# Four more weight pieces begun in the first five attention groups of an attention, expert and MLP kernel on Trainium2

## Chip, core and metric

The kernel runs on one NeuronCore of a Trainium2 chip (trn2). The metric is the device time of one execution in microseconds (us). Of the kernel before there are three timed runs: 333.08, 333.13 and 334.42 us, median 333.13 us.

## What is computed

Three steps follow each other. All inputs are float32.

```python
def _attn_ref(q, k, v, mem_k, mem_v):          # q, k, v: 4 x 8 heads x 768 x 64
    ...
    chunk, left_ctx, right_ctx = (32, 16, 8)    # 24 chunks of 32 queries, each sees
    ...                                         # 8 memory keys + its own 56 neighbours
        a = softmax(scale * q_c @ k_full.T)
        out[:, :, c_start:c_end] = a @ v_full

def _moe_ref(x, phi, w1, w2):                   # x: 3072 x 512, 8 experts, 4 slots each
    logits = x @ phi
    slot_input = softmax(logits, 0).T @ x       # 32 x 512, needs every token
    slot_out[e] = relu(slot_input[e] @ w1[e]) @ w2[e]     # 512 -> 1024 -> 512
    return softmax(logits, 1) @ slot_out

def _moe2_ref(x, w_in, w_out, g_ln):            # 512 -> 1024 -> 512
    h = x @ w_in
    solu = h * softmax(h)
    return (layernorm(solu) * g_ln) @ w_out
```

## The kernel before

**Attention, 32 groups.** `GROUPS` is 32: four batches, two halves of the sequence, four pairs of heads. The loop over `g` (lines 842 to 874) takes one group per turn. Its keys and queries come as one tile, `kq` (128 x 800, four buffers), its values as two transfers into `vz` (64 x 780 each, four buffers). `emit_spread` copies keys and memory keys into a padded tile `kz` on POOL, with a part on ACT (line 303 is POOL's copy), then TensorE (PE) multiplies queries and keys (line 254), DVE and ACT make the softmax, PE turns it (line 292) and multiplies by the values (line 310). Every fourth group the logits and the running weighted sum for the expert slots are brought up to date. After the last group some merging follows (lines 875 to 912), and only then is the input of the experts known.

**Experts, 32 units.** The loop over `units` (lines 931 to 951) goes through `w1` and `w2` of the eight experts in halves. A unit uses two pieces of 512 KB: eight matmuls at line 497 (`w1`) or at line 515 (`w2`). Between them lie the turn of the hidden values (line 504), a sum on DVE (507) and a relu on ACT (508).

**Last stage.** The 32 slot outputs go through `w_in`, and then 24 tiles of 128 tokens through SoLU, layer norm and `w_out`. Its main matmuls are at line 723.

**Weight pieces.** `chunks` lists 80 pieces of 512 KB in the order of loading: eight of `w_in` (line 234, into `e` areas) alternating with seven of `w_out` (line 234, into `w` areas), then the 64 of the experts (line 231), then the last of `w_out`. `load_e(n)` begins at most `n` more of them, as far as slots are free. A slot of `w_in` becomes free when a cast on POOL (line 592, one of five steps of a cast that is spread over the groups from g = 3 to 30) has read it. When the attention ends, the areas of `kq`, `vz` and of the token tiles become 13 more slots (`ex` areas). From then on a slot becomes free when a unit has used it (`release`, line 941).

**The queue.** Every load is issued by SyncE (SP), in program order: `load_qk(g + 4)`, `load_e(LOADS[g])`, `load_v(g + 3)` in each group. An issue waits until its buffer is free, and everything behind it waits too. SP also has a limit on the transfers under way, as its waits for earlier transfers in the trace show. `LOADS` (line 45) gives the number of pieces per group.

```python
            if g + 4 < GROUPS:
                load_qk(g + 4)
            load_e(LOADS[g])
            if 1 <= g:
                emit_pv(g - 1)
            if g + VLEAD < GROUPS:
                load_v(g + VLEAD)
```

Of the kernel before, what the change touches and what calls it, by code (L numbers as in the profile page):

```python
# [41 lines left out]
NE = 25  # L42
CAST0, CASTN, NEARLY = 3, 3.4, 8
VLEAD = 3
LOADS = [0] + [1, 1, 1, 0] + [1] * 28
LANE, SIDE = 2.6, 1

CASTU = (0, 1, 2, 3, 4, 5, 6)
# [31 lines left out]
def tile_kernel(ctx: ExitStack, tc: tile.TileContext, kr, vr, w1, w2, w_in, w_out, cst, out):  # L80
# [106 lines left out]
    def load_qk(g):  # L187
        sp.dma_start(out=kq[g % 4], in_=kr[g])
# [30 lines left out]
    def load_e(n=99):  # L219
        while n and nxt[0] < len(chunks):  # L220
            key = chunks[nxt[0]]
            if key[0] == "wout":
                slot = wslot[key[1]]
            elif free:
                slot = free.pop(0)
            else:
                break
            slot_of[key] = slot
            if key[0] in ("w1", "w2"):
                src = (w1 if key[0] == "w1" else w2)[key[1], key[2]]  # L230
                sp.dma_start(out=slot.rearrange("p (k f) -> p k f", k=2), in_=src)
            else:
                src = (w_in if key[0] == "win" else w_out)[key[1]]
                sp.dma_start(out=slot.bitcast(I64), in_=src)
            nxt[0] += 1
            n -= 1
# [561 lines left out]
    with tc.manual_schedule():  # L798
# [42 lines left out]
        for g in range(GROUPS):  # L841
# [6 lines left out]
# [4 lines that stand above are left out]
# [207 lines left out]
```

## Time and profile before

| what | value |
|---|---|
| timed runs, median of 3 | 333.13 us |
| profiled execution, its own time | 334.36 us |
| its span in the trace | 332.5 us |
| granted TensorE clock, mean | 0.999 of full speed |
| busy: PE, DVE, ACT, POOL | 90%, 72%, 67%, 51% of the span |
| moved by the DMA engines | 95.86 MB, mean 288 GB/s |
| chain that ended last | PE 56%, DMA 32%, DVE 5% of the span |

The span is the part between the first and the last instruction; 1.86 us of the profiled execution lie around it. Times in rows are microseconds from the span's start. A share of busy time says little here, since the kernel has stages with different limits: the rows further down are read by stage. The GB/s of a stretch is what all 16 DMA engines moved in it.

### The profile page before, as it was taken

How to read it: one execution, taken by the hardware profiler on the slowest of the kernel's cores; microseconds unless marked ns; L12 is line 12 of the kernel's file. 1: busy time of each engine (PE TensorE's matmuls, PEld its weight loads, DVE VectorE, ACT ScalarE, POOL GpSimd, SP SyncE). 2: the span in 40 equal slices, each digit the busy share in tenths (PEclk: the TensorE clock that was granted, in tenths of full speed). 3: DMA queues.
4: the chain of work that ended last, by engine and by line, in shares of the span. 5: the costliest groups of instructions: out<-in, count | busy, mean ns of one | idle time of the engine just before them, and what ended most of it. 6: DMA issues, size and time to landing. Idle time of an engine off the chain costs nothing.

```text
span 332.5 us, 8398 instructions
## 1 busy us (share of the span) xinstructions
PE 300.8 (90%) x3069; PEld 218.1 (66%) x3069; DVE 239.4 (72%) x432; ACT 223.1 (67%) x441; POOL 169.9 (51%) x398
## 2 busy tenths in 40 slices
PE   2979698897897789888999999999999999999996
PEld 2667576675675533332434788888888888888885
DVE  6686887797768438999117886897888778787540
ACT  3476656764765427685524779998888888888721
POOL 5436567566767023222100357777767677676600
PEclk9999999999999999999999999999999999999999
DMA  7999999999999999999950004667666756666531
GB/s 286 366 359 405 407 399 411 412 411 414 409 407 396 418 417 419 415 421 416 417 228 0 0 34 158 252 206 264 207 244 211 246 209 201 240 231 234 202 95 64
DMA packets 39433, 95.86 MB, mean 288 GB/s; under 512 B 4832, under 2 KB 15456, under 8 KB 39392
## 3 DMA queue, kind: packets, MB, share of 16 engines
q1 hardware_dynamic: 39248, 95.11, 75.3%
q8 instruction: 24, 0.39, 0.5%
q10 hardware_dynamic: 144, 0.22, 0.2%
q14 instruction: 17, 0.14, 0.1%
HBM read 78.53 MB, written 16.78 MB: 287 GB/s over the span
## 4 chain that ended last, share of the span: by engine, by line
PE 56%; DMA 32%; DVE 5%; ACT 2%; issue 2%; POOL 1%; SPq 1%; ACTq 0%; POOLq 0%
PE bank L723 37%; DMA kq_area<-in_kr_dram 19%; DMA ex_area<-in_w_dram 6%; DMA e_area<-in_w_dram 6%; PE h L635 4%; PE bank L254 3%; PE bank L310 2%; PE bank L497 1%; POOL kq_area L303 1%; PE bank L292 1%; DMA vz_area<-in_vr_dram 1%; PE bank L515 1%; PE bank L733 1%; PE t L733 1%; PE t L692 1%
## 5 line engine op out<-in xcount | busy, mean ns | idle before, releaser
L723 PE MATMUL bank<-wh_area,yh_area 128*128 128x512 f32 x552 | 129.8, 390 | 0.0
L723 PEld LDWEIGHTS bank<-wh_area,yh_area 128*128 128x128 f32 x552 | 103.4, 188 | 21.8
L303 POOL TENSOR_SCALAR kq_area<-kq_area 64x416 f32<-64x416 f32 x88 | 38.5, 443 | 38.5 <-DMA kq_area<-in_kr_dram 27.9
L254 PE MATMUL bank<-kq_area 128*32 128x128 f32 x768 | 29.8, 293 | 16.8 <-POOL kq_area L303 10.8
L706 DVE STREAM_TRANSPOSE yq_area<-yq_area 128x1024 f32<-128x1024 f32 x20 | 24.9, 1246 | 17.2 <-DMA yq_area<-z 17.2
L254 PEld LDWEIGHTS bank<-kq_area 128*32 128x32 f32 x768 | 21.0, 116 | 23.1 <-POOL kq_area L303 15.2
L650 DVE SCALAR_TENSOR_TENSOR eb_area<-h,eb_area 128x1024 f32<-128x1024 f32 x24 | 29.0, 1213 | 9.2 <-ACT eb_area L644 9.0
L295 ACT COPY s_area<-bank 128x384 f32<-128x384 f32 x32 | 15.2, 476 | 27.7 <-PE bank L292 26.1
L310 PE MATMUL bank<-vz_area,s_area 128*32 128x130 f32 x768 | 29.7, 279 | 2.2 <-ACT s_area L295 1.6
L272 DVE TENSOR_REDUCE cst_area<-bank 128x6 f32<-128x384 f32 x32 | 17.7, 554 | 19.2 <-PE bank L254 19.0
L688 POOL TENSOR_SCALAR cst_area<-cst_area 128x1 f32<-128x1 f32 x72 | 26.6, 369 | 7.6
L641 DVE TENSOR_REDUCE cst_area<-h 128x1 f32<-128x1024 f32 x24 | 29.0, 1216 | 0.9 <-PE h L635 0.9
L644 ACT ACTIVATE eb_area<-h,cst_area 128x1024 f32<-128x1024 f32 x24 | 26.6, 1110 | 1.9 <-DVE cst_area L641 1.9
L673 ACT ACTIVATE eb_area<-eb_area,cst_area 128x1024 f32<-128x1024 f32 x24 | 27.3, 1138 | 0.1
L677 POOL TENSOR_SCALAR cst_area<-cst_area 128x1 f32<-128x1 f32 x24 | 15.9, 662 | 21.7 <-ACT eb_area L644 19.8
L717 DVE TENSOR_TENSOR yh_area<-yq_area,yh_area 128x1024 fp32r<-128x1024 f32 x20 | 24.5, 1224 | 2.3 <-ACT yh_area L713 2.3
L670 ACT ACTIVATE eb_area<-eb_area,cst_area 128x1024 f32<-128x1024 f32 x20 | 23.1, 1155 | 4.3 <-DVE eb_area L650 3.8
L310 PEld LDWEIGHTS bank<-vz_area,s_area 128*32 128x32 f32 x768 | 22.3, 111 | 5.0 <-ACT s_area L295 2.8
L689 POOL TENSOR_SCALAR cst_area<-cst_area 128x1 f32<-128x1 f32 x72 | 21.9, 304 | 7.1
L713 ACT CAST yh_area<-yq_area 128x1024 fp32r<-128x1024 f32 x20 | 21.0, 1049 | 6.3 <-DVE yq_area L706 6.3
L741 ACT ACTIVATE eb_area<-bank,cst_area 128x512 f32<-128x512 f32 x23 | 15.8, 685 | 8.8 <-POOL cst_area L679 5.9
L299 ACT COPY kq_area<-kq_area 64x416 f32<-64x416 f32 (+1 forms) x34 | 12.2, 407 | 11.2 <-DMA kq_area<-in_kr_dram 11.1
(154 smaller groups left out, 534.2 us busy)
## 6 DMA issues: line engine op xcount, KB each, us to landing
e_area<-in_w_dram SPq DMA_DIRECT2D x37, 512.0 KB, 8.5
ex_area<-in_w_dram SPq DMA_DIRECT2D x26, 512.0 KB, 10.0
kq_area<-in_kr_dram SPq DMA_DIRECT2D x32, 400.0 KB, 6.3
vz_area<-in_vr_dram SPq DMA_DIRECT2D x64, 195.0 KB, 6.3
z<-eb_area SPq DMA_DIRECT2D x20, 512.0 KB, 2.7
yq_area<-z SPq DMA_DIRECT2D x80, 128.0 KB, 2.9
out_dram<-eb_area SPq DMA_DIRECT2D x23, 256.0 KB, 2.1
e_area<-in_w_in_dram SPq DMA_DIRECT2D x8, 512.0 KB, 6.4
```

The costliest lines, as they stand in the source:

```text
L254: pe.matmul(out=bk[32 * j:32 * j + 32, t * 128:(t + 1) * 128], lhsT=kq[i][:, KT + c * CH:KT + (c + 1) * CH], rhs=kwin(g % 2, c), start=Tru ...
L303: pool.tensor_scalar(out=o, in0=i, scalar1=1.0, scalar2=0.0, op0=ALU.mult, op1=ALU.add)
L310: pe.matmul(out=bk[32 * j:32 * j + 32, t * 2 * VW:(t + 1) * 2 * VW], lhsT=atb[g % 2][:, c * CH:(c + 1) * CH], rhs=vz[g % 4][:, :, c * VW:( ...
L641: dve.tensor_reduce(out=sc("nm", i), in_=fin["h"][i % 2], axis=AX.X, op=ALU.max, negate=True)
L644: act.activation(out=eb[i % FIN], in_=fin["h"][i % 2], func=ACTF.Exp, bias=sc("nm", i), accum_out=sc("s", i))
L650: dve.scalar_tensor_tensor(out=ub[i % FIN], in0=fin["h"][i % 2], scalar=-1.0 / FF, in1=eb[i % FIN], op0=ALU.mult, op1=ALU.mult, accum_out= ...
L670: act.activation(out=yb[i % FIN], in_=ub[i % FIN], func=ACTF.Identity, scale=-float(FF), bias=sc("nu", i))
L673: act.activation(out=sq, in_=ub[i % FIN], func=ACTF.Square, scale=-float(FF), bias=sc("nu", i), accum_out=sc("vs", i))
L688: pool.tensor_scalar(out=t, in0=r, scalar1=r, scalar2=xx, op0=ALU.mult, op1=ALU.mult)
L706: dve.transpose(out=yv[i % FIN].rearrange("p (f a t) -> p a f t", f=FC, a=4), in_=yq[i % FIN].rearrange("p (a f t) -> p a f t", f=FC, a=4),)
L717: dve.tensor_tensor(out=yl[i % FIN][:, sl], in0=tps(i, sl) if i < NPE else yv[i % FIN], in1=yh[i % FIN][:, sl].bitcast(FP32), op=ALU.subtract,
L723: pe.matmul(out=fin["o"][i % 2], lhsT=a[i % FIN][:, f * 128:(f + 1) * 128], rhs=w[f], start=start, stop=stop)
```

## The change

Only the table `LOADS` changes. Counted from g = 0, the groups g = 1, 2 and 3 begin two pieces each in place of one, and g = 4 begins one in place of none. All later groups begin one as before, so that each piece comes four places earlier in the loop, 34 pieces are asked for in the loop in place of 30, and four fewer are left for after it. No other engine's order changes.

```diff
-LOADS = [0] + [1, 1, 1, 0] + [1] * 28
+LOADS = [0, 2, 2, 2] + [1] * 28
```

SP's queue at the groups g = 1 to 3, before (`e1` is the area of `w_in` pieces, `w0` of a `w_out` piece; `kq` and `vz` belong to groups four and three ahead):

```order
L234 DMA e1_area_73<-in_w_in_dram 128x512
L202 DMA vz_area_71<-in_vr_dram 64x780 x2
L188 DMA kq_area_70<-in_kr_dram 128x800
L234 DMA w0_area_76<-in_w_out_dram 128x512
L202 DMA vz_area_71<-in_vr_dram 64x780 x2
L188 DMA kq_area_70<-in_kr_dram 128x800
L234 DMA e1_area_73<-in_w_in_dram 128x512
```

and with the change:

```order
L234 DMA e1_area_73<-in_w_in_dram 128x512
L234 DMA w0_area_76<-in_w_out_dram 128x512
L202 DMA vz_area_71<-in_vr_dram 64x780 x2
L188 DMA kq_area_70<-in_kr_dram 128x800
L234 DMA e1_area_73<-in_w_in_dram 128x512
L234 DMA w1_area_77<-in_w_out_dram 128x512
L202 DMA vz_area_71<-in_vr_dram 64x780 x2
L188 DMA kq_area_70<-in_kr_dram 128x800
L234 DMA e1_area_73<-in_w_in_dram 128x512
```

In both excerpts the rows of `kq` are the keys of g = 6 and g = 7. Ahead of the keys of g = 6 now stand two pieces in place of one, ahead of those of g = 7 four in place of two.

SP's queue at the end of the attention, from the keys of the last group on, before (`e1`, `e2` are slots that `w_in` pieces had, `ex0` is the area of `kq`):

```order
L188 DMA kq_area_70<-in_kr_dram 128x800
L231 DMA e1_area_73<-in_w2_dram 128x1024
L202 DMA vz_area_71<-in_vr_dram 64x780 x2
L231 DMA e1_area_73<-in_w2_dram 128x1024
L202 DMA vz_area_71<-in_vr_dram 64x780 x2
L231 DMA e1_area_73<-in_w1_dram 128x1024 x2
L231 DMA e2_area_74<-in_w2_dram 128x1024 x2
L231 DMA e2_area_74<-in_w1_dram 128x1024 x2
L231 DMA ex0_area_1696<-in_w2_dram 128x1024 x2
```

and with the change:

```order
L188 DMA kq_area_70<-in_kr_dram 128x800
L231 DMA e2_area_74<-in_w2_dram 128x1024
L202 DMA vz_area_71<-in_vr_dram 64x780 x2
L231 DMA e2_area_74<-in_w2_dram 128x1024
L202 DMA vz_area_71<-in_vr_dram 64x780 x2
L231 DMA e2_area_74<-in_w1_dram 128x1024 x2
L231 DMA ex0_area_1700<-in_w2_dram 128x1024 x2
```

Behind the last keys stand four pieces for slots that are free already or soon, before eight: the other four now lie ahead of these keys. The pieces from `ex0` on have the same places after as before.

## Rows read from the trace of the kernel before

**Rows 1.** The page, what the DMA engines moved, in 40 slices of 8.3 us

```profile
GB/s 286 366 359 405 407 399 411 412 411 414 409 407 396 418 417 419 415 421 416 417 228 0 0 34 158 252 206 264 207 244 211 246 209 201 240 231 234 202 95 64
```

**Rows 2.** Busy time by stretch; last: granted clock, DMA share, GB/s

```profile
14.00:22.00 8.00, 7.74 (x191) 6.15 (x183) 6.18 (x17) 5.89 (x15) 2.40 (x6) 1.00 0.94 317
22.00:100.00 78.00, 66.83 (x1464) 52.31 (x1459) 60.92 (x156) 50.78 (x140) 50.62 (x90) 1.00 1.03 408
...
123.00:166.00 43.00, 38.87 (x312) 14.22 (x305) 32.99 (x73) 28.85 (x68) 11.62 (x13) 1.00 1.03 418
```

**Rows 3.** The chain that ended last, in order of time: start, us, what

```profile
42.86 5.62 DMA kq_area<-in_kr_dram
...
87.79 7.04 DMA kq_area<-in_kr_dram
...
161.61 9.74 DMA e_area<-in_w_dram
171.40 1.05 PE bank L515 x4
```

**Rows 4.** The page's DMA issues: KB each, median us to landing

```profile
kq_area<-in_kr_dram SPq DMA_DIRECT2D x32, 400.0 KB, 6.3
vz_area<-in_vr_dram SPq DMA_DIRECT2D x64, 195.0 KB, 6.3
```

**Rows 5.** SP's queue in order of time, from 9 to 18 us: start, us

```profile
9.63 0.43 SPq L234 DMA_DIRECT2D e_area<-in_w_in_dram  x1
12.88 1.12 SPq L202 DMA_DIRECT2D vz_area<-in_vr_dram  x2
...
17.49 0.43 SPq L234 DMA_DIRECT2D e_area<-in_w_in_dram  x1
```

**Rows 6.** DMA issues at 0.72, 9.63 and 17.49 us; last: us to landing

```profile
kq_area<-in_kr_dram SPq DMA_DIRECT2D x1, 400.0 KB, 4.0
...
e_area<-in_w_in_dram SPq DMA_DIRECT2D x1, 512.0 KB, 5.4
...
e_area<-in_w_in_dram SPq DMA_DIRECT2D x1, 512.0 KB, 7.2
```

**Rows 7.** POOL and PE in order of time, end of attention and first expert unit

```profile
101.36 2.12 POOL L303 TENSOR_SCALAR kq_area<-kq_area 64x416 f32<-64x416 f32 x4 [0.23 <-DMA kq_area<-in_kr_dram]
103.57 1.31 POOL L592 TENSOR_TENSOR cst_area<-e_area,cst_area 128x512 f32<-128x512 f32 x1
...
122.31 1.92 PE L497 MATMUL bank<-e_area,cst_area 128*32 128x512 f32 x16 [0.27 <-DVE cst_area L426]
```

**Rows 8.** SP's queue in order of time: three issues that waited for a slot

```profile
104.91 0.33 SPq L231 DMA_DIRECT2D e_area<-in_w_dram  x1
...
123.40 0.80 SPq L231 DMA_DIRECT2D e_area<-in_w_dram  x2
...
129.91 1.28 SPq L231 DMA_DIRECT2D e_area<-in_w_dram  x3
```

**Rows 9.** DMA issues at 104.91, 123.40 and 129.91 us; last: us to landing

```profile
e_area<-in_w_dram SPq DMA_DIRECT2D x1, 512.0 KB, 8.8
...
e_area<-in_w_dram SPq DMA_DIRECT2D x1, 512.0 KB, 7.7
...
e_area<-in_w_dram SPq DMA_DIRECT2D x1, 512.0 KB, 7.4
```

**Rows 10.** PE by line, 122 to 172 us: busy, mean ns, idle before

```profile
L515 PE MATMUL bank<-e_area,hr_area 128*32 128x512 f32 x76 | 12.7, 604 | 0.9 <-ACT hr_area L508 0.5 <-DMA e_area<-in_w_dram 0.2
```

**Rows 11.** All engines in order of time, the last expert units

```profile
163.87 1.07 PE L515 MATMUL bank<-ex_area,hr_area 128*32 128x512 f32 x8
...
168.04 1.97 PE L515 MATMUL bank<-e_area,hr_area 128*32 128x512 f32 x8
...
168.40 0.22 ACT L508 ACTIVATE hr_area<-hr_area 128x16 f32<-128x16 f32 x1 [1.51 <-DVE hr_area L507]
...
170.24 2.21 PE L515 MATMUL bank<-e_area,hr_area 128*32 128x512 f32 x8 [0.24 <-DMA e_area<-in_w_dram]
```

## The prediction

> **What bounds the kernel now.** I read the page's slices first: the DMA engines move some 410 GB/s from the fourth slice to the twentieth, then nothing, and after that only the last stage's own traffic [rows 1]. So there are two parts: up to about 171 us the loads run at one level, behind them PE works alone. The chain that ended last says the same: in the attention it consists of transfers of `kq` one behind the other, in the expert units of weight pieces, up to a piece issued at 161.61 us that lands 9.74 us later, at 171.35; the four matmuls that wait for it end at 171.40 + 1.05 = 172.45 us [rows 3]. Behind 172.45 us neither the order nor the loads change, so I take these 332.5 - 172.45 = 160.1 us as fixed and ask only when the last expert unit ends.
>
> Next I read the DMA rate by stretch. From 22 to 100 us it is 408 GB/s, from 123 to 166 us 418, but from 14 to 22 us only 317 [rows 2]. That is the gap into which the four pieces are put. SP shows its cause: it issues a `w_in` piece at 9.63 us, waits, and issues the next transfers only at 12.88 us [rows 5], so that few are under way afterwards.
>
> Third, whether the expert units wait for loads. From 122 to 172 us the group of line 515 idled 0.2 us for a transfer [rows 10]. Inside units 31 and 32 it did wait: eight matmuls take 1.07 us in an undisturbed unit, here 1.97 and 2.21 us, and the second starts 2.20 us after the first [rows 11]. So the units run at the engines' own pace almost to the end and meet the loads only in the last two. Two ends lie close together, and the change moves them in opposite directions.
>
> **Part 1: the attention gets later.** A group of the loop loads 400 KB of keys, 2 x 195 KB of values [rows 4] and 512 KB of a piece [rows 6], 1302 KB. In the chain, `kq` transfers follow from the issue at 42.86 us to the landing of that issued at 87.79 us, at 94.83 us: eight links, each from the keys of one group to those of the group two further, 16 groups in 51.97 us, 3.25 us per group [rows 3]. One piece therefore costs 512 / 1302 x 3.25 = 1.28 us of the loads, and four more pieces ahead of the last keys 5.1 us. From this goes what the gap gives back, which I call y. The spread of the last keys on POOL begins at 101.36 us, 0.23 us after POOL is free, when the keys have landed [rows 7]; from there to the first expert unit at 122.31 us is a chain of compute, so that unit begins 5.1 - y later.
>
> **Part 2: what the gap gives back.** The old profile doesn't show this, so I bound it. Below: the deeper queue helps nothing, y = 0. By the rate: 8 us at 317 in place of 408 GB/s are 8 x 91 / 408 = 1.8 us. By landings: the piece issued at 9.63 us lands after 5.4 us, at 15.0; that issued at 17.49 us after 7.2 us, at 24.7 [rows 5, 6]. Between them are two groups' loads, worth 2 x 3.25 = 6.5 us, and they took 9.7: 3.2 us lost. A landing counts the slowest of 16 engines and a rate their mean, hence the two figures; the attention waits for landings, but part of their delay may be slow single transfers that a longer queue doesn't cure. I take 2.4 us, just under the middle of 1.8 and 3.2; the ends are 0 and 3.2.
>
> So the expert units begin 5.1 - 2.4 = 2.7 us later.
>
> **A rule that speaks against it.** The row of 408 GB/s was said above [rows 2]. The Trainium skill, page "DMA: Bandwidth & Descriptors", section "Bandwidth", holds that between HBM and SBUF the memory's share of about 358 GB/s per core binds. By that the gap would give back only 8 x (358 - 317) / 358 = 0.9 us. The end would then be 5.1 - 0.9 - 2.3 = +1.9 us by the steps below. The trace disagrees: two long stretches lie at 408 and 418 GB/s, so the sum stays with the rows.
>
> **Part 3: the compute end of the units.** With no wait for a load, the unit that begins at 168.04 us would end after 1.07 us, at 169.11; the relu that the last unit needs is done at 168.62 us, so the last would end at 170.18 us [rows 11]. Against 172.45 us that is 2.3 us of room. A start 2.7 us later uses it up: the end by compute is 2.7 - 2.3 = 0.4 us later than now.
>
> **Part 4: the load end of the units.** Left alone, the loads are earlier by y, 2.4 us. But three issues wait for compute: one at 104.91 us for the cast of a `w_in` piece on POOL, which ends at 104.88; one at 123.40 us for the first unit; one at 129.91 us for the sixth [rows 7, 8]. They move 2.7 us back while the queue ahead of them drains 2.4 us sooner, which takes 5.1 us from the reserve of each. The reserve is what the piece had to stand in line for: it landed 8.8, 7.7 and 7.4 us after issue [rows 9]. A first transfer of 400 KB with nothing ahead took 4.0 us [rows 6]; 112 KB more at the above pace add 0.3. So the reserves are 4.5, 3.4 and 3.1 us; the smallest lets 5.1 - 3.1 = 2.0 us of idle loads arise in all (idle time at an earlier one counts towards the next). The load end is 2.0 - 2.4 = -0.4 us: earlier than now. Issuing costs SP 0.43 us per piece [rows 5], the same pieces as before, only elsewhere.
>
> The places of PE, DVE, ACT and POOL in their queues don't change. Their waits inside the attention grow with the keys' delay and are part of the 2.7 us already. Slots of `w_in` pieces are asked for four places earlier; the last of them is the wait at 104.91 us, costed above.
>
> **The sum.** The later of the two ends counts: +0.4 us. The profiled execution took 334.36 us, 1.86 us of them around its span, and would take 334.8. That execution stands 1.2 us above the median of 333.13, so against the median I forecast 333.13 + 0.4 = **333.5 us**. A measurement of this kernel can tell about 0.5%, 1.7 us, from no change.
>
> **Rivals.**
> - *The attention is simply pushed back* (slower). If the gap is no lack of queued work, y is near 0 and the units begin up to 5.1 us later: 5.1 - 2.3 = +2.8 us, 335.9. It decides from y below 1.1, where the end passes +1.7. For it: at 17.49 us a piece already takes 7.2 us to land, so something was queued, and the DMA share was 0.94 [rows 2, 6]. Against: the rate climbs to 408 with the same mix of transfers. Chance 0.10.
> - *The gap has a ceiling of its own* (slower). If the rate there rises only halfway, to 362 GB/s, y is 8 x 45 / 362 = 1.0 and the end 5.1 - 1.0 - 2.3 = +1.8 us, 334.9. For it speaks the high DMA share at the low rate, against it the 408 GB/s right behind [rows 2]: chance 0.03. The Trainium skill's page "DMA: Bandwidth & Descriptors" would put such a ceiling near 358 GB/s.
> - *The loads are the end after all, by the slot waits.* If a piece needs 5.4 us to land even with little ahead, as the one at 9.63 us did [rows 6], the smallest reserve is 7.4 - 5.4 = 2.0 us, the idle loads are 3.1 us and the end is 3.1 - 2.4 = +0.7 us, 333.8. Chance 0.17.
> - *The gap is filled entirely* (earlier). With y = 3.2 the units begin 1.9 us later, inside their room: 1.9 - 2.3 = -0.4 us by compute, 2.0 - 3.2 = -1.2 by loads; 332.7. To be over 0.5% faster both ends would have to move 1.7 us, for which the units would also need over a microsecond more room than the rows show. Chance 0.18, of which 0.04 over 0.5%.
> - *Nothing is begun earlier*, because SP comes to its limit of transfers under way at once. Then SP waits where it issued before, and the time is within 0.3 us of 333.1. Against: between 9.63 and 12.88 us SP waits for the multiplication by the values, not for transfers. Chance 0.05.
>
> The forecast's own case has 0.47.
>
> **How the numbers follow.** The first two rivals are slower by over 0.5%, 0.04 of the fourth is faster by that, all else lies within it: faster 0.04, same 0.83, slower 0.13. The range reaches from the full gap, 332.7, less 0.4 us (the next unit's matmuls may begin before the last of a unit has ended, so the room of 2.3 us is a lower bound), up to +2.1 us, y = 0.7, which leaves out most of the first rival: 332.3 to 335.2.
>
> **What would show it.** Right: from 14 to 22 us over 380 GB/s; the first unit of line 497 begins near 125.0 us; units 31 and 32 take close to 1.07 us each; the last matmul of line 515 ends near 172.9; PE's last stage is as long as before. Rival one: the gap's rate stays near 317 and the first unit begins at 126 us or later. The slot waits: a dip of the rate around 127 to 136 us, and the last units still wait for a piece. Wrong altogether: a last stage of another length, or an attention end that doesn't move with the landing of the last keys.

## The result and the profile after

| kernel | time, median | ratio to before | 95% interval |
|---|---|---|---|
| before | 333.12 us | | |
| the change | 336.31 us | 1.0088 | 1.0063 to 1.0114 |

The change is slower by 0.88%, 2.9 us, by the ratio; the two medians lie 3.2 us apart. Forecast was +0.4 us, 333.5 us in 332.3 to 335.2, with 0.13 on slower: the forecast and its range missed. The first rival's +2.8 us comes nearest.

The profiled execution of the change took 336.94 us, its span 335.1 us. First two rows of the page's 40 slices: the granted clock of PE in tenths, and what the DMA engines moved, as in [rows 1].

```profile
PEclk9999999999999997999999999999999999999999
...
GB/s 290 388 412 388 404 410 412 413 412 405 393 406 406 372 415 334 373 413 420 416 291 0 0 33 156 226 216 248 228 245 192 236 219 206 247 216 236 213 90 64
```

The loads are low in three slices of 8.4 us that were near 415 before, those of 372, 334 and 373 GB/s (109 to 117 us and 126 to 142 us). By stretch, in the columns of [rows 2]:

```profile
14.00:22.00 8.00, 5.07 (x112) 3.76 (x108) 4.15 (x12) 3.26 (x8) 2.40 (x6) 1.00 1.02 408
22.00:100.00 78.00, 63.66 (x1421) 50.03 (x1421) 59.09 (x151) 50.29 (x136) 47.12 (x84) 1.00 1.03 405
106.00:110.00 4.00, 2.68 (x64) 2.23 (x68) 3.62 (x11) 2.02 (x9) 3.71 (x6) 1.00 0.92 343
126.00:130.00 4.00, 4.00 (x24) 0.99 (x20) 0.06 (x1) 2.22 (x4) 1.25 (x1) 0.62 0.80 293
123.00:166.00 43.00, 38.16 (x286) 13.79 (x289) 34.02 (x77) 27.39 (x63) 12.39 (x13) 0.96 0.99 392
```

The stretch of 14 to 22 us is full, 408 in place of 317 GB/s, as forecast. Behind the attention the rate falls to 343 and 293 GB/s, and from 123 to 166 us it is 392 in place of 418. What SP waited for there is told by its wait groups from 100 to 140 us (total, times, longest, in us):

```profile
SPq L231 <- PE bank L497: 8.8, 4, 6.7
SPq L231 <- PE bank L515: 4.3, 2, 3.7
SPq L231 <- POOL cst_area L592: 3.5, 1, 3.5
SPq L231 <- PE bank L310: 3.4, 1, 3.4
```

The first three rows hold the three slot waits of [rows 8]: for the first unit, for the sixth, for a cast of a `w_in` piece on POOL. The fourth, for the last multiplication by the values, stands ahead of an `ex` piece issued at 115.47 us; the prediction did not count it. Next POOL, then PE, in order of time (answering to [rows 7] and [rows 11]):

```profile
105.00 1.03 POOL L303 TENSOR_SCALAR kq_area<-kq_area 64x416 f32<-64x416 f32 x2 [0.40 <-PE bank L310]
...
168.82 1.07 PE L515 MATMUL bank<-ex_area,hr_area 128*32 128x512 f32 x8
...
171.26 1.07 PE L515 MATMUL bank<-e_area,hr_area 128*32 128x512 f32 x8
...
172.84 2.20 PE L515 MATMUL bank<-e_area,hr_area 128*32 128x512 f32 x16
```

and three links of the chain that ended last (answering to [rows 3]):

```profile
98.46 6.39 DMA kq_area<-in_kr_dram
...
125.60 3.61 PE bank L497 x16
...
172.91 2.13 PE bank L515 x16
```

The last keys land at 98.46 + 6.39 = 104.85 us, and POOL begins to spread them at 105.00, 3.6 us later than at 101.36 [rows 7]. The first unit begins at 125.60 us, 3.3 us later than at 122.31 [rows 7]. Its 16 matmuls take 3.61 us in place of 1.92: the granted clock in 126 to 130 us is 0.62 of 2.4 GHz, so part of that stretch ran at the lower level, 1.2 GHz. The units behind 168.82 and 171.26 us take 1.07 us each, the last two together 2.20: none waits for a load any more, and the last matmul of line 515 ends at 172.91 + 2.13 = 175.04 us, 2.6 us behind 172.45 [rows 3]. The stage behind it lasts 335.1 - 175.04 = 160.1 us, as before.

### The profile page after: what moved, and what is told of

Read it like the earlier page. It is cut to its first block, busy times and chain, and to the rows that moved or that the text cites. A ratio compares the mean times of both kernels' runs of the same rounds, so it can differ in the third digit from the quotient of the medians.

```text
span 335.1 us, 8396 instructions
## 1 busy us (share of the span) xinstructions
PE 297.7 (89%) x3069; PEld 216.1 (64%) x3069; DVE 238.8 (71%) x432; ACT 223.6 (67%) x441; POOL 170.9 (51%) x398
## 4 chain that ended last, share of the span: by engine, by line
PE 55%; DMA 26%; DVE 13%; ACT 2%; issue 2%; POOL 1%; SPq 1%; POOLq 0%; ACTq 0%; DVEq 0%
PE bank L723 36%; DMA kq_area<-in_kr_dram 23%; PE h L635 4%; DMA w_area<-in_w_out_dram 3%; PE bank L497 2%; PE bank L515 2%; POOL kq_area L303 1%; DVE wo_area L586 1%; PE bank L504 1%; PE bank L254 1%; DVE wh_area L616 1%; DVE wo_area L595 1%; DVE cst_area L592 1%; DVE cst_area L589 1%; PE bank L310 1%
## 5 line engine op out<-in xcount | busy, mean ns | idle before, releaser
L254 PE MATMUL bank<-kq_area 128*32 128x128 f32 x768 | 29.1, 286 | 22.1 <-POOL kq_area L303 14.9
L254 PEld LDWEIGHTS bank<-kq_area 128*32 128x32 f32 x768 | 20.3, 113 | 28.5 <-POOL kq_area L303 20.1
L272 DVE TENSOR_REDUCE cst_area<-bank 128x6 f32<-128x384 f32 x32 | 17.7, 554 | 23.1 <-PE bank L254 22.9
L295 ACT COPY s_area<-bank 128x384 f32<-128x384 f32 x32 | 15.2, 476 | 24.9 <-PE bank L292 23.4
L688 POOL TENSOR_SCALAR cst_area<-cst_area 128x1 f32<-128x1 f32 x72 | 27.5, 382 | 7.6
L310 PE MATMUL bank<-vz_area,s_area 128*32 128x130 f32 x768 | 27.8, 274 | 2.9 <-ACT s_area L295 2.1
L677 POOL TENSOR_SCALAR cst_area<-cst_area 128x1 f32<-128x1 f32 x24 | 19.0, 793 | 19.3 <-ACT eb_area L644 17.4
L310 PEld LDWEIGHTS bank<-vz_area,s_area 128*32 128x32 f32 x768 | 21.3, 108 | 5.1 <-ACT s_area L295 3.5
L689 POOL TENSOR_SCALAR cst_area<-cst_area 128x1 f32<-128x1 f32 x72 | 20.2, 281 | 7.1
```

The lines of the kernel that those rows point to most:

```text
L254: pe.matmul(out=bk[32 * j:32 * j + 32, t * 128:(t + 1) * 128], lhsT=kq[i][:, KT + c * CH:KT + (c + 1) * CH], rhs=kwin(g % 2, c), start=Tru ...
L310: pe.matmul(out=bk[32 * j:32 * j + 32, t * 2 * VW:(t + 1) * 2 * VW], lhsT=atb[g % 2][:, c * CH:(c + 1) * CH], rhs=vz[g % 4][:, :, c * VW:( ...
L688: pool.tensor_scalar(out=t, in0=r, scalar1=r, scalar2=xx, op0=ALU.mult, op1=ALU.mult)
```

## The experiments

After the result there were three theories. *Push-back*: the pieces ahead of the last keys cost what they weigh, and the filled gap gives little back. *The clock*: the fall at the first unit makes the difference. *The slot waits*: the loads ran dry at the three waits. A ratio is to the kernel before, timed in the same rounds; the third run of the kernel before has none.

**The kernel before, again, and a third time.** No edit.

> The kernel before once more, for the granted clock of each of its runs (the table of the runs before shows none). Theory C (most of what a run of the change loses beyond 1.6 us is TensorE at its lower clock level for a few us at the first expert units): here the clock is 0.997 or more in nearly every run and the runs lie within 333 to 334.5 us. Rival (the clock falls as often here, and is not what differs): clocks of 0.985 to 0.995 in half of the runs.

> The kernel before a third time, one look. Theory that the gap of 14 to 22 us belongs to single executions: the rate there is near 400 GB/s when this execution takes 333 us or less, near 320 to 350 GB/s when it takes 334 us or more. Theory that it is always there: under 350 GB/s whatever the time.

Measured: ratio 0.998 [0.9956, 1.0003] for the first. Nine of its twelve timed executions had a mean clock of 0.999 or 1.0 and three 0.99 or 0.995, so the clock falls here too, but in fewer of them than the rival asked for. Both profiled executions took 332.48 and 332.49 us, where the one that the prediction read took 334.36. Stretches of the first of them:

```profile
14.00:22.00 8.00, 6.96 (x159) 5.25 (x152) 6.23 (x19) 5.27 (x12) 2.64 (x7) 1.00 1.03 402
...
106.00:123.00 17.00, 14.07 (x146) 7.73 (x141) 6.30 (x21) 5.98 (x21) 2.15 (x2) 1.00 1.03 417
123.00:166.00 43.00, 38.83 (x310) 14.19 (x309) 33.25 (x74) 28.62 (x68) 10.66 (x12) 1.00 1.03 418
```

its chain:

```profile
120.79 1.92 PE bank L497 x16
...
159.73 9.75 DMA e_area<-in_w_dram
169.52 1.05 PE bank L515 x4
```

and SP's queue in order of time:

```profile
9.63 0.43 SPq L234 DMA_DIRECT2D e_area<-in_w_in_dram  x1
11.52 1.12 SPq L202 DMA_DIRECT2D vz_area<-in_vr_dram  x2
```

The stretch of the other:

```profile
14.00:22.00 8.00, 6.66 (x159) 5.15 (x152) 6.26 (x19) 5.27 (x12) 2.64 (x7) 1.00 1.03 387
```

What follows: the gap belongs to single executions. Where SP issues again at 11.52 us, the stretch has 402 GB/s; where it does so only at 12.88 us, 317 [rows 2, 5]. Against these two executions the units of the profiled one began 1.5 us late (122.31 against 120.79) and it ended 1.9 us late. The medians of the kernel before, 333.12 to 333.93 us from round to round, lie between the two kinds.

PE's rows show where the two part. SP's issue waits for the first multiplication by the values (line 310). In the profiled execution of [rows 5] it ran at

```profile
11.29 1.53 PE L310 MATMUL bank<-vz_area,s_area 128*32 128x130 f32 x24
```

and ended at 12.82 us; in the kernel before, again, at

```profile
10.59 0.87 PE L310 MATMUL bank<-vz_area,s_area 128*32 128x130 f32 x24
```

and ended at 11.46 us. SP issues 0.06 us behind either end. The same 24 matmuls take 1.55 us in a stretch of the lower clock level (the kernel with two more pieces, further down, from 26.81 us):

```profile
26.81 1.55 PE L310 MATMUL bank<-vz_area,s_area 128*32 128x130 f32 x24
```

So TensorE still ran at the lower level, 1.2 GHz, in the first execution, and already at the higher one in the second. The column of the granted clock doesn't show this: the trace's first record of the clock, at full speed, begins at 14.57 us in the one and at 9.74 us in the other, and the column counts a stretch without a record as full. Over the 14 profiled executions of this case, whatever the kernel, that record begins at 8.4 to 9.9 us in eight, at 11.5 in one and at 14.3 to 15.2 in five. Why it comes late in some isn't shown.

**The changed kernel again.** No edit.

> The changed kernel a second time, to see another execution of it. Median 336.3 us by every theory. Theory of the clock (a stretch at half clock costs the units up to 1.7 us): executions with a mean granted clock of 0.997 or less lie a microsecond or more above those at 0.999 or more, and if this profile has no stretch below full clock, the first unit of line 497 takes 1.92 us and the last unit ends about 173.4 us. Theory of the push-back (the loads ahead of the last keys cost what they weigh and the clock costs little): times and clocks do not go together, the last keys land 3.5 to 5 us later than in either execution of the kernel before (101.22, 100.03), and the last unit ends near 174.5 to 175 us with or without a fall.

Measured: 335.77 us, ratio 1.0086 [1.0054, 1.0119]. Of the timed executions those at a mean clock of 1.0 took 335.53, 335.54 and 336.01 us, those at 0.995 took 335.43, 335.52 and 337.08, two at 0.99 took 338.49 and 338.83. Stretches of its profile, the clock in the column before the last two:

```profile
14.00:22.00 8.00, 6.01 (x133) 4.47 (x132) 4.89 (x15) 4.17 (x10) 2.40 (x6) 1.00 1.03 413
...
106.00:112.00 6.00, 5.36 (x113) 4.09 (x114) 4.61 (x13) 2.64 (x8) 3.18 (x4) 1.00 0.91 339
123.00:140.00 17.00, 15.66 (x126) 6.02 (x125) 12.11 (x30) 11.19 (x26) 5.38 (x5) 1.00 0.99 386
```

and its chain:

```profile
124.93 1.92 PE bank L497 x16
...
162.62 9.82 DMA e_area<-in_w_dram
172.48 1.05 PE bank L515 x4
```

What follows: without a clock fall at the units (it fell earlier, in the attention) the loss is still there, as push-back said. The units begin 124.93 - 120.79 = 4.1 us later than in the undisturbed kernel before, and end 172.48 + 1.05 - (169.52 + 1.05) = 3.0 us later, waiting for a weight piece. The fall that the first profile shows adds to this in single executions: 173.53 us is nearer to the 173.4 that the theory of the clock gave for the end of the units than to push-back's 174.5 to 175, and the two executions at 0.99 took some 3 us more.

**Filling the gap with nothing pushed back, twice.** Both keep 30 pieces in the loop; the first leaves four groups in a row empty near its end, the second four groups five apart.

```diff
-LOADS = [0] + [1, 1, 1, 0] + [1] * 28
+LOADS = [0, 2, 2, 2] + [1] * 18 + [0] * 4 + [1] * 6
```

> The early part of the change alone: two pieces in g = 1 to 3 and one in g = 4, but none in g = 22 to 25, so that 25 pieces stand ahead of the last keys as before, and 30 in the loop. Theory P (the four pieces push the last keys back, less what the gap gives back, 1.0 to 1.5 us by landings): the last keys land 1.0 to 1.5 us earlier than before, at 99.7 to 100.2 us, the first unit begins near 121 us, and the time is 0.5 to 1.5 us below before. Rival Q (the bunch of early pieces disturbs the DMA engines, whose first and last landing of a transfer stood 3.1 us apart behind it, and that is what costs): last keys no earlier than before, time 0.5 to 1.5 us above before.

```diff
-LOADS = [0] + [1, 1, 1, 0] + [1] * 28
+LOADS = [0, 2, 2, 2] + [1, 1, 1, 1, 0] * 4 + [1] * 8
```

> The early groups as in the change, and four groups later on, five apart, begin no piece, so that the loads ahead of the last keys weigh what they weighed before. If the kernel before has the gap of 14 to 22 us in every execution: keys land 1.2 to 2.4 us earlier and so do the units, 331 to 332 us. If the gap was an accident of the one profiled execution (the second profile of the same kernel has 402 GB/s there): nothing to gain, last keys at 100 to 101 us, 333.0 to 333.8 us. If it is the doubled pieces in early groups themselves that cost (they starve the attention early, PE's clock falls): 334.5 us or more with the last keys still near 101 us.

Measured: the first 335.74 us, ratio 1.0066 [1.0045, 1.0087]; the second 333.83, ratio 1.0004 [0.9978, 1.003]. Stretches of the first:

```profile
14.00:22.00 8.00, 5.80 (x132) 4.34 (x127) 4.71 (x14) 4.03 (x9) 2.41 (x6) 1.00 1.03 414
...
90.00:106.00 16.00, 14.61 (x334) 11.32 (x330) 14.19 (x37) 11.57 (x34) 14.57 (x23) 1.00 0.95 335
```

What follows: by its time the first is slower even than the rival had it, and the first theory missed, but the cause is another than either said: four empty groups in a row only move the hole. From 90 to 106 us the loads run at 335 GB/s, which against 410 is 16 x 75 / 410 = 2.9 us of loads, and 2.2 us come out as time. Spread out, the hole is gone and the time is that of before: within the interval, 0.7 us less to 1.0 us more, the double early pieces do no harm by themselves, and filling the stretch of 14 to 22 us gains nothing in the median.

**How many pieces: two, three, four late ones, two fewer.** With the change (four) and the kernel before (none) they make a curve.

```diff
-LOADS = [0] + [1, 1, 1, 0] + [1] * 28
+LOADS = [0, 2, 2, 1, 0] + [1] * 28
```

> Half of the change: two extra pieces ahead of the last keys in place of four. Theory of the push-back with the forecast's room of 2.3 us behind the attention: 2 x 1.28 = 2.6 us later, inside the room but for 0.3 us, 333.5 to 333.9 us. Push-back without room (the end follows the last keys): half of the +3.2 us that four pieces cost, 334.6 to 335.2 us. The gap of 14 to 22 us is there in every execution and is filled by two pieces: 2.6 - 2.4 = 0.2 us, 333.0 to 333.4 us.

```diff
-LOADS = [0] + [1, 1, 1, 0] + [1] * 28
+LOADS = [0, 2, 2, 2, 0] + [1] * 28
```

> Three extra pieces. Theory of a room and then a slope (two pieces cost nothing, four cost 2.4 us): past the room each piece costs its 1.28 us on the loads, so 1.0 to 1.6 us, 334.9 to 335.5 us. Theory that it is the fourth piece (the filled group 5) that does the harm: as with two, within 0.5 us of the kernel before.

```diff
-LOADS = [0] + [1, 1, 1, 0] + [1] * 28
+LOADS = [0] + [1, 1, 1, 0] + [1] * 17 + [2] * 4 + [1] * 6
```

> The other part alone: the early groups as before, but two pieces in place of one in g = 22 to 25, so that 29 pieces stand ahead of the last keys as with the change. Theory P: the last keys land a full 5.1 us later than before, near 106.3 us, first unit near 127 us, and the time is 2.5 to 4 us above before, about 1 us above the change. Rival Q: the time is within 0.7 us of before, since the early groups are untouched.

```diff
-LOADS = [0] + [1, 1, 1, 0] + [1] * 28
+LOADS = [0] + [1, 1, 1, 0] + [1] * 8 + [0] + [1] * 7 + [0] + [1] * 11
```

> The other side: two groups in the middle begin no piece, so that the attention gets its last keys 2.6 us earlier and the weights stand behind. Theory that the loads' total is the end on this side: the units begin at 118.2 to 119.7 us, the last unit still ends when the last piece lands, within 0.5 us of the kernel before (333.4 to 334.4 us). Theory that the attention's end sets the time on both sides: 2 us or more faster, near 331.5 us.

| pieces more ahead of the last keys | ratio | 95% interval | first unit, profile |
|---|---|---|---|
| -2 | 1.0016 | 0.9992 to 1.0039 | (121.50) |
| 0 | 0.998 | 0.9956 to 1.0003 | 120.79 |
| 2 | 0.9993 | 0.9974 to 1.0011 | 122.60 |
| 3 | 1.0024 | 0.9994 to 1.0054 | 123.84 |
| 4, early (the change) | 1.0086 | 1.0054 to 1.0119 | 124.93 |
| 4, late | 1.0135 | 1.0089 to 1.018 | none |

(The profiled execution of the kernel with four late pieces ran at a mean granted clock of 0.85 and says nothing of its units.)

The chain of the kernel with two more pieces shows where the room ends:

```profile
122.60 1.92 PE bank L497 x16
...
168.28 1.98 PE bank L515 x16
```

Its units run from 122.60 to 168.28 + 1.98 = 170.26 us without waiting for a load at the end, 47.7 us. In the kernel before they take 169.52 + 1.05 - 120.79 = 49.8 us: the room is 2.1 us, and two pieces, which push the first unit back by 1.8 us, fit into it. What follows: the time is flat from two fewer to two more and rises beyond. Two fewer gain nothing, as the theory of the loads' total had it, but their units began at 121.50 us, not at its 118.2 to 119.7, so that the end on that side isn't shown. Three came to 334.44 us, between the two theories, and their interval still takes in the time of before. The bend lies near three pieces rather than two. Four late pieces cost 1.35%, 4.5 us, more than the 2.5 to 4 expected; that is 1.6 us more than four early ones, with intervals that overlap.

The profiled execution of the kernel with two fewer pieces was a late one (span 335.6 us). It has the gap as well, with PE's row of 11.29 us again at 1.53 us, and a second hole, 304 GB/s from 100 to 106 us; so the gap is only a part of its length. Its stretch:

```profile
14.00:22.00 8.00, 7.70 (x183) 6.12 (x171) 6.01 (x17) 5.66 (x15) 2.41 (x6) 1.00 0.94 320
```

and SP's queue, whose next issue again comes only at 12.88 us:

```profile
12.88 1.12 SPq L202 DMA_DIRECT2D vz_area<-in_vr_dram  x2
```

This answers to the gap of [rows 2, 5] in a second kernel; its first unit, at 121.50 us, is therefore in brackets above.

**The clock, held up.** The change with two more warming matmuls at each of the two places in the chain between the last keys and the first unit.

```diff
-TKEEP = [2, 1]
+TKEEP = [4, 3]
```

> The change, with two more idle matmuls of 384 columns at each of the two places ahead of the first expert units where the kernel already has such matmuls (4 and 3 in place of 2 and 1). Theory C: the clock is 0.997 or more in nearly every run, the runs lie together near 334.8 us, 1.5 us below the change. Rival (the scatter of the change has another cause): median 336.3 us and a scatter of 3 us as before, or 0.3 us more for the added matmuls.

Measured: 337.81 us, ratio 1.0125 [1.0087, 1.0162], against 1.0088 of the change. First POOL's spread of the last keys, then PE's row of warming matmuls and the first unit, in order of time:

```profile
103.89 2.06 POOL L303 TENSOR_SCALAR kq_area<-kq_area 64x416 f32<-64x416 f32 x4 [0.38 <-DMA kq_area<-in_kr_dram]
...
119.02 2.83 PE L527 MATMUL bank<-s_area,cst_area 128*128 128x384 f32 x8
...
123.43 2.18 PE L527 MATMUL bank<-s_area,cst_area 128*128 128x384 f32 x6
...
126.81 1.92 PE L497 MATMUL bank<-e_area,cst_area 128*32 128x512 f32 x16 [0.27 <-DVE cst_area L426]
```

The first unit ran at full clock, 1.92 us. But from the spread to it passed 126.81 - 103.89 = 22.9 us, against 125.60 - 105.00 = 20.6 in the change: the warming matmuls lay on the path and cost more than the fall. A miss for the clock theory as put, and no clean test of it; the changed kernel's second profile is the better one. A clock fall in the attention costs nothing that can be seen: in the kernel with two more pieces 11 of 12 timed executions had a mean clock of 0.995 or less, and their median is that of before. Its profile has the fall early in the attention:

```profile
24.00:26.00 2.00, 0.19 (x8) 0.19 (x12) 0.07 (x2) 0.44 (x2) 1.59 (x4) 1.00 1.05 418
26.00:30.00 4.00, 4.00 (x66) 3.35 (x62) 1.84 (x5) 1.44 (x4) 1.59 (x5) 0.57 1.04 417
```

**The first slot wait, taken away.** The change, with the casts of the early `w_in` pieces one group earlier, and then spaced so that the last of them stands ahead of the last keys' spread in POOL's queue.

```diff
-CAST0, CASTN, NEARLY = 3, 3.4, 8
+CAST0, CASTN, NEARLY = 2, 3.4, 8
```

> The change, with the casts of the early w_in pieces one group earlier, so that the slot for which SP waits until about 108.6 us in the change is free one group, some 3 us, earlier. Theory of the slot waits (the load end is late because the queue drained at them): the rate from 106 to 123 us rises from 389 to above 405 GB/s, the last weight piece lands up to 1 us earlier, 335.3 to 335.8 us. Theory that the attention's end alone sets it: the same as the change, 336.0 to 336.6 us.

```diff
-CAST0, CASTN, NEARLY = 3, 3.4, 8
+CAST0, CASTN, NEARLY = 2, 3.1, 8
```

> The change, with the casts of the early w_in pieces spaced so that the last of them stands ahead of the spread of the last keys in POOL's order (with one group earlier it still stood behind). SP's first wait, at 104 to 108 us in the change, should be gone, and the rate from 106 to 112 us rise from some 340 to above 400 GB/s. Theory of the slot waits: the idle loads there (about 1 us) come back at the end, 334.8 to 335.3 us. Theory that the later waits on the first and sixth unit take it up: 335.6 to 336.2 us, as the change.

Measured: 335.55 us, ratio 1.0075 [1.0048, 1.0103], and 335.44 us, ratio 1.0071 [1.0043, 1.01]. The first moved nothing that matters: the last cast still stood behind the last keys' spread, and its 106 to 112 us were still at 335 GB/s. The second did what it should; its stretches:

```profile
106.00:112.00 6.00, 5.40 (x112) 3.87 (x101) 3.50 (x10) 1.85 (x7) 0.34 (x1) 1.00 1.03 404
123.00:140.00 17.00, 15.71 (x125) 6.01 (x124) 12.11 (x30) 11.14 (x26) 5.39 (x5) 1.00 0.93 361
```

What follows: the first hole is gone, 404 in place of 339 GB/s, and the second is deeper, 361 in place of 386. The loads that no longer run dry at the cast run dry at the first unit instead; the time is that of the change within the intervals. That the first lies inside the 335.3 to 335.8 us of the slot-wait theory is luck: its rate from 106 to 123 us was 383 GB/s, not above 405. One wait taken away is no gain while a later one on the same queue is due to the same delay.

These two executions show one thing more. In both the clock rose late (14.7 and 14.4 us) and SP's issue came at 12.88 us, yet the stretch behind it is full; the second:

```profile
14.00:22.00 8.00, 7.74 (x199) 6.35 (x191) 6.63 (x19) 6.42 (x16) 2.42 (x6) 1.00 1.02 403
```

and its chain:

```profile
124.99 1.92 PE bank L497 x16
```

The first has 390 GB/s there and begins its first unit at 125.54 us. So where an execution has the late start, the early pieces do fill the gap.

## Why the prediction was wrong

**The step that failed is Part 2, y = 2.4 us, as a figure for the median.** It took the gap of 14 to 22 us for a property of the kernel. It belonged to an execution in which TensorE came to its full clock late: the two others of the same kernel have 402 and 387 GB/s there, against 413 in the second profile of the change. By the prediction's own formula that is worth 8 x 11 / 413 = 0.2 to 8 x 26 / 413 = 0.5 us. By the start of the units, 5.1 - 4.1 = 1.0 us. So y is 0.2 to 1.0 us where the clock rises early. That the spread version gained nothing in the median agrees with this.

**The last line of the sum counted the gap twice.** The forecast noted that the profiled execution stood 1.2 us above the median and then took its +0.4 us over to the median. But part of what made that execution long was what y was to give back. How many executions have the gap, and so how much of it the median holds, isn't shown. Against executions of its own kind y was about right: the first unit was forecast at 125.0 us and began at 124.99 and 125.54 us in the two versions with other casts, whose clock also rose late, so 5.1 - 2.7 = 2.4 and 5.1 - 3.2 = 1.9 us came back. Their spans are 0.9 and 1.4 us longer, where +0.4 was forecast. That the two profiles of the change itself, with an early clock, also began near 125.0 us (124.93 and 125.60) is luck: they are to be counted from 120.79, not from 122.31. The last unit ended at 173.53 us in the second profile, where 172.9 was forecast.

**Part 1 holds.** Four pieces weigh 5.1 us; 4.1 us of them arrive at the first unit, and two pieces give 1.8 of 2.6 us.

**Part 3 holds in its room,** 2.1 us measured, 2.3 forecast. With a start 4.1 us later the compute end is 4.1 - 2.1 = +2.0 us. The clock fall of the first profile adds 3.61 - 1.92 = 1.7 us in that execution.

**Part 4 had the mechanism, but too little idle time.** The end that decides is this one, +3.0 us in the second profile, not the compute end. The idle loads were forecast at 2.0 us. Against the kernel before, again, they are 6 x (418 - 339) / 418 = 1.1 us from 106 to 112 us, 11 x (417 - 408) / 417 = 0.2 from 112 to 123, 17 x (417 - 386) / 417 = 1.3 from 123 to 140 and 26 x (419 - 416) / 419 = 0.2 from 140 to 166: 2.8 us. With y = 2.4 even these would have moved the end by only 0.4 us; with y at 0.2 to 0.5 they move it by 2.3 to 2.6. The piece that the last unit waits for landed 3.0 us later (162.62 + 9.82 against 159.73 + 9.75). The rest is its landing: the last of the 16 engines finished it 1.8 us after their mean, against 1.3 us in the kernel before, again, by the trace's records of landings.

**The rivals.** The first, *the attention is simply pushed back*, gave +2.8 us, and +2.9 was measured. But it expected the stretch to stay at 317 GB/s, and it filled. Its y near 0 was right for another reason, and in the second profile the end was set by the loads (+3.0) and not by compute (+2.0), so the third rival's slot waits were at work; that its sum fits is in part luck. The rule of the Trainium skill, page "DMA: Bandwidth & Descriptors", section "Bandwidth", would have given +1.9 us, nearer than my sum. The section gives that share of 358 GB/s for two cores that load at once, which the prediction left out. No stretch here bears it out for this core: the filled one ran at 408 and 413 GB/s in the two profiles of the change.

**The signs that the prediction named** held in the first profile of the change for the stretch over 380 GB/s, for the unit start, for the pace of the last two units (2.20 / 2 = 1.1 us) and for the last stage's length, and not for the end of line 515. The dip that it named for the slot waits, 127 to 136 us, was there as well, and in the second profile the last unit waited for a piece. None of the signs asked whether the gap was there in another execution of the kernel before.

## What to carry to other kernels

A profile is one execution. Where its time lies above the median, ask first which of its stretches makes it so, and don't credit a change with mending that stretch. A loss that only some executions have is in the median in part or not at all: look at a second profile of the same kernel before pricing a gap. Compare the times of the same matmuls too, and not the clock's column alone, which here stood at 1.00 over a stretch at the lower level. Where two ends lie close together, moving work from one queue position to an earlier one is free only up to the room between them (here two pieces of 512 KB), and beyond it the waits on that queue behind the delayed stage came due one after the other.

## What the runs showed that was not expected

One unchanged program can run its first 20 us in two ways, by when TensorE comes to its full clock: at 9.74 us in one execution and at 14.57 us in another. The first multiplication by the values then takes 0.87 or 1.53 us, SP's next issue comes at 11.52 or 12.88 us, 402 or 317 GB/s follow, and the whole took 332.48 or 334.36 us. The two executions differ in other things too, so not all of the 1.9 us need come from this.

The granted clock fell to the lower level between 22 and 100 us in six of the nine profiled executions of kernels whose early groups begin two pieces, and in none of the three of the kernel before. With two more pieces PE had been busy for 0.19 of the 2 us before, its mean clock was then 0.57 in 26 to 30 us, and the time stayed that of before: from 20 to 60 us the chain that ended last consists almost wholly of transfers there. At the first expert unit, where other work waits for PE, a fall made 1.92 us into 3.61.
